# One bias group a step later, squares on ScalarE, and transposes of normalized rows moved beside the next tile's

## The chip, the core and the metric

The kernel runs on one core of a Trainium2 chip. The metric is the device time of one execution in microseconds (us). The kernel before takes 612.4 us, the median of three runs (612.08 to 612.52).

## The reference, cut to what matters

```python
scores = q @ k.T / sqrt(64)                       # (2, 8, 576, 576)
bias = relu(log1p(|i-j|) / log1p(max(i,1)) * w1 + b1) @ w2      # one per head
attn = softmax(scores + bias); x = attn @ v       # -> (1152, 512)
x = x / sqrt(mean(x*x, -1) + 1e-6) * rms_g
y = (silu(x @ w_gate) * (x @ w_val)) @ w_out      # weights in float64, cut to float32
out = (s * relu(y @ w_in)**2 + b) @ w_out2
```

## The kernel before

The instruction order of every engine is written by hand: each engine runs its own list in the order in which the Python code issues it, and waits only on semaphores. The attention stage is a loop over steps `s`. One step handles one unit, which is one pair of heads of one tile of 128 query rows; there are 9 tiles of 4 units (`r = s % 4`), so 36 units. The feed-forward layers come after it and take the larger part of the time.

In step `s` TensorE (PE) computes, in this order: the bias rows of one group of 16 query positions (`bias_mm`, line 188; a group is due some steps ahead of its use), the scores of unit `s+1` (line 243), three batches of transposes of the probabilities of unit `s` (`turn_mm`, called t0, t1 and t2 here, lines 271 and 273), the products of unit `s-1` with the values (line 300), and at certain `r` the transposes of a finished tile. VectorE (DVE) does the softmax sums (`soft`, line 255), the copy of t1 (line 279) and most hidden rows of the bias network (`hidden`, line 175). ScalarE (ACT) does the exponentials (line 262), the copies of t0 and t2 (line 279) and the bias rows (`br`, line 204), which travel through DRAM (`rows`) into the `bias` tile of a chunk of query positions.

A finished tile `p` passes these functions: `finish_a` copies the attention output out of PSUM (oT, line 306), `finish_t` transposes it on PE into a PSUM bank (line 313), `finish_b` scales it on VectorE by the softmax sums (ri, lines 319 and 320; x, line 322), `finish_s` sums its squares and takes the power -0.5 (lines 330 and 334), `finish_n` normalizes (line 339), and `finish_c` transposes the normalized rows on PE into a PSUM bank (line 345), from which ScalarE casts the high part `xs[0]` (line 348) and VectorE then subtracts to get the low part `xs[1]` (line 349). In the loop, `finish_a` and `finish_t` of tile `p` come at `r = 1`, `finish_b` and `finish_s` at `r = 2` of the next step, `finish_n` at `r = 3`, `finish_c` at `r = 0`.

All PSUM tiles named `b` come from one ring of three banks, in the order in which they are asked for; the bias rows of groups 8 and up, t0, t1, t2, and the two transposes of a finished tile share it. A fourth request takes the first one's bank again and has to wait until that one has been read:

```python
psB = ring(ctx, "psB", 3, space=PSUM)
```

Groups 32 to 35 have rows of over 512 columns and take two banks each; from step 25 on there are no bias groups any more.

Of the kernel before, what the change touches and what calls it, by code (L numbers as in the profile page):

```python
# [12 lines left out]
AF = mybir.ActivationFunctionType  # L13
ALU = mybir.AluOpType
# [9 lines left out]
NTT = 9  # L24
NT = B * S
DM = H * D
# [7 lines left out]
TILES = list(range(NTT))  # L34
POOL_QUAD = 3
ACT_QUAD = 2
ACT_EARLY = (0, 1, 2, 3, 4, 5, 6, 7, 10, 11)
SCALE = 8.0
AHD = 8
POOL_FROM = 12  # L40
# [10 lines left out]
def tile_kernel(ctx: ExitStack, tc: tile.TileContext, q, k, v, ltab, lg, cst, cst2, rms_g, wg, wv, wo, win, wo2, s_p, b_p, out):  # L51
    nc = tc.nc
# [70 lines left out]
    def load_q(p):  # L123
        if p < NTT:
            qt[p] = q_p.tile([P, NP, P], F32, name="q")
            nc.sync.dma_start(out=qt[p], in_=q[TILES[p]])

    def load_k(n):
        ks[n] = ac.tile([P, S], F32, name=f"ks{n}")
        nc.sync.dma_start(out=ks[n], in_=k[:, n])  # L130

    def load_v(n):
        t = ac.tile([P, 10, D], F32, name=f"vs{n}")
        nc.sync.dma_start(out=t, in_=v[:, n])
        vs[n] = t
# [10 lines left out]
    def keep_clock(n):  # L146
        warm = psB.tile([P, 512], F32, name="b")
        for _ in range(n):
            nc.tensor.matmul(warm[:, :P], ident, ident, start=True, stop=True)
# [13 lines left out]
    def hidden(g):  # L163
        hms[g] = []
        d = reach(g)
        for tq in range(4):
# [3 lines left out]
            hms[g].append(hq)  # L170
            if tq == ACT_QUAD and g in ACT_EARLY:
                nc.scalar.activation(hq, src, AF.Relu, bias=nthr[:, n:n + 1], scale=w1_sb)
# [19 lines left out]
    def bias_out(g, pb):  # L192
# [10 lines left out]
        for dst, src in parts:  # L203
            nc.scalar.activation(dst, src, AF.Identity, bias=cb[:, 1:2] if g in ACT_EARLY else cb[:, 0:1],  # L204
                                 scale=minv_sb[:, g:g + 1])
# [8 lines left out]
    def bias_in(g):  # L214
        qc, g16 = divmod(g, 8)
        if qc not in bias:
            bias[qc] = bias_p.tile([P, H, S], F32, name="bias")
        r = rows.pop(g)
        src = bass.AP(tensor=r.tensor, offset=r.offset + 15, ap=[[H * RW - 1, 16], [RW, H], [1, S]])
        for dst in ([0] if qc < 4 else [0, 64]):  # L220
            to = dst + (P if qc < 4 else D)
            nc.sync.dma_start(out=bias[qc][dst + g16:to:8 if qc < 4 else 4, :, :], in_=src)
# [11 lines left out]
    def scores_mm(u):  # L234
        hp = u % 4
        ps = [psA.tile([P, 2, 512], F32, name="a").rearrange("p f c -> p (f c)")[:, 512 - SPLIT:512 - SPLIT + S]
              for _ in range(2)]
        b = batches(u)
        for f in (slice(0, SPLIT), slice(SPLIT, S)):
            for e in range(2):  # L240
                for i in range(2):
                    ed, qc = slice(e * D, (e + 1) * D), slice(i * D, (i + 1) * D)
                    nc.tensor.matmul(ps[e][qc, f], qt[u // 4][ed, hp, qc], ks[b[i % len(b)] * NP + hp][ed, f],  # L243
                                     start=True, stop=True, tile_position=(e * D, i * D))
        return ps
# [58 lines left out]
    def finish_a(p):  # L304
        oT = xx_p.tile([P, DM], F32, name="oT")
        nc.scalar.copy(oT, pos.pop(p))
        fin[p] = oT

    def finish_t(p):
        oT = fin[p]  # L310
        px = psB.tile([P, 512], F32, name="b")
        for c in range(NKC):
            nc.tensor.transpose(px[:, c * P:(c + 1) * P], oT[:, c * P:(c + 1) * P], ident)
        fin[p] = oT, px

    def finish_b(p):
        oT, px = fin[p]
        ri = st_p.tile([P, H], F32, name="ri")
        nc.vector.tensor_scalar(ri, sums.pop(p), 1e-9, None, op0=ALU.add)
        nc.vector.reciprocal(ri, ri)  # L320
        x = xx_p.tile([P, DM], F32, name="x")
        nc.vector.tensor_tensor(out=x.rearrange("p (h d) -> p h d", h=H),
                                in0=px.rearrange("p (h d) -> p h d", h=H),
                                in1=ri.unsqueeze(2).to_broadcast([P, H, D]), op=ALU.mult)
        fin[p] = oT, x

    def finish_s(p):
        oT, x = fin[p]
        ss = st_p.tile([P, 1], F32, name="ss")
        nc.vector.tensor_tensor_reduce(out=oT, in0=x, in1=x, scale=1.0 / DM, scalar=1e-6,  # L330
                                       op0=ALU.mult, op1=ALU.add, accum_out=ss)

        rstd = st_p.tile([P, 1], F32, name="rstd")
        nc.gpsimd.tensor_tensor(out=rstd, in0=ss, in1=mh, op=ALU.pow)
        fin[p] = x, rstd
# [5 lines left out]
    def finish_c(p):  # L341
        x = fin.pop(p)[0]
        pxt = psB.tile([P, 512], F32, name="b")
        for c in range(NKC):
            nc.tensor.transpose(pxt[:, c * P:(c + 1) * P], x[:, c * P:(c + 1) * P], ident)
        src = pxt.rearrange("p (c t) -> p c t", c=NKC)
        cs = slice(p * P, (p + 1) * P)
        nc.scalar.copy(xs[0][:, :, cs], src)
        nc.vector.tensor_tensor(out=xs[1][:, :, cs], in0=src, in1=xs[0][:, :, cs].bitcast(F32), op=ALU.subtract)
# [28 lines left out]
    def bits_of(n):  # L378
        raw, a = wst[n]
        w = wst[n] = wpools["ab"].tile([P, 4 * P], I32, name="ww")  # L380
        yield nc.vector.tensor_scalar(a, a, 3, 0x3FFFFFF8, op0=ALU.logical_shift_left, op1=ALU.bitwise_and)  # L381
        yield nc.vector.scalar_tensor_tensor(out=w, in0=raw[:, :, 1], scalar=-0x40000000, in1=a,  # L382
                                             op0=ALU.bitwise_and, op1=ALU.bitwise_or)
        yield nc.vector.scalar_tensor_tensor(out=w, in0=raw[:, :, 0], scalar=29, in1=w,  # L384
                                             op0=ALU.logical_shift_right, op1=ALU.bitwise_or)
# [15 lines left out]
    NU = 4 * NTT  # L401
    NG = S // 16
    plan = {s: [] for s in range(-2, NU + 4)}
    plan[-2] = list(range(AHD))
    for g in range(AHD, NG):
        plan[g - 11 if g > 11 else -1].append(g)

    def hide(g):
        if g < NG:
            hidden(g)  # L410
# [12 lines left out]
    def groups(s):  # L423
        for g in plan[s]:
            pb = bias_mm(g)
            bias_out(g, pb)
            if s == -1 and g == AHD:
                hide(11)
            if s == -2:
                hide(g + LEAD)  # L430

    for s in range(-2, NU + 1):
        r = s % 4
        if s >= 5 and r == 1:
            finish_a(s // 4 - 1)
        if s >= 0 and r == 0:
            load_q(s // 4 + 1)
        if -1 <= s < 5:
            load_k(s + 3)
        if 0 <= s < 7:  # L440
            load_v(s + 1)
        landed = list(rows)[:2 if s > 3 else 1]
        if s != -1:
            groups(s)
        for g in landed:
            bias_in(g)
        if s >= 6 and r == 2:
            finish_b(s // 4 - 1)
        if s in BITS:
            part = bits_of(BITS[s])  # L450
        if 0 <= s + 1 < NU:
            ps = scores_mm(s + 1)
            if s == -1:
                groups(s)
                keep_clock(3)
            soft(s + 1, 0, ps[0])
        next(part, None)
        if 0 <= s < NU:
            turn_out(s, 0, turn_mm(s, 0))
        if 0 <= s + 1 < NU:  # L460
            expo(s + 1, 0)
            soft(s + 1, 1, ps[1])
        next(part, None)
        if 0 <= s < NU:
            for e in (1, 2):
                turn_out(s, e, turn_mm(s, e))
        if 0 <= s + 1 < NU:
            expo(s + 1, 1)
        next(part, None)
        if s >= 6 and r == 2:  # L470
            finish_s(s // 4 - 1)
        if s >= 7 and r == 3:
            finish_n(s // 4 - 1)
        if s >= -1:
            hide(s + 13)
        if s == 4:
            nc.sync.dma_start(out=s_sb, in_=s_p)
            nc.sync.dma_start(out=b_sb, in_=b_p)
        if 0 <= s - 1 < NU:
            values_mm(s - 1)  # L480
        if s >= 5 and r == 1:
            finish_t(s // 4 - 1)
        if s == 6:
            xs = [act_p.tile([P, NKC, NT], F32R, name=f"xs{i}", tag=f"x{i}") for i in range(2)]
        if s >= 8 and r == 0:
            finish_c(s // 4 - 2)
        if s == 26:
            gen.close()
            wpools["ab"] = ring(ctx, "wab", 2)
            wpools["sp"] = ring(ctx, "wsp", 4)  # L490
        for at, fn, n in TAIL:
            if at == s:
                fn(n)
        if s == 34:
            sco.close()
            psC = ring(ctx, "psC", 4, space=PSUM)
# [255 lines left out]
```

## Time and profile before

| what | value |
|---|---|
| median of three runs | 612.4 us (612.08 to 612.52) |
| profiled execution | 612.25 us, span of its instructions 610.5 us |
| granted TensorE clock | 1.00 of full speed |
| PE busy | 602.0 us (99% of the span) |
| VectorE, ScalarE, GpSimd busy | 407.8, 310.0, 191.2 us |
| start-up to the first t0 | 0 to 26.3 us |
| attention steps | 26.3 to about 180.4 us |
| feed-forward layers | 180.4 us to the end |

The span goes from the first to the last instruction; 1.75 us of the execution lie outside it. A busy PE says little by itself, since ends of matmuls are modelled; when each instruction starts says more. The idle time in square brackets in a timeline row is that of the engine just before the instruction, with what ended it.

### The profile page before, as it was taken

To read this page: it belongs to the slowest core of one execution; us is meant where nothing else is said; L and a number is where in the kernel's file an instruction comes from. 1 tells how busy PE (TensorE), PEld (TensorE's weight loads), DVE (VectorE), ACT (ScalarE), POOL (GpSimd) and SP (SyncE) were. 2 spreads that over 40 slices of the span, in tenths; PEclk is the share of its full clock that TensorE was granted. 3 is DMA by queue.
4 is the path that set the end of the run, shared out by engine and by line. 5 is a ranking of instruction groups with operands and counts; after the bars stand their busy time and mean duration, and the time that the engine had idled before them with its cause. 6 is when DMAs were issued, how large, how long until landed. Compare 5 with 4: busy or idle time off the path is not lost.

```text
span 610.5 us, 13370 instructions
## 1 busy us (share of the span) xinstructions
PE 602.0 (99%) x5430; PEld 540.2 (88%) x5430; DVE 407.8 (67%) x750; ACT 310.0 (51%) x646; POOL 191.2 (31%) x176
## 2 busy tenths in 40 slices
PE   8999999999999999999999999999999999999997
PEld 6466666667789999999999999999999999999997
DVE  7977999977878545654556355447887635788841
ACT  7887777777764443444434222335554335555210
POOL 0424235620113333234324223323224323332420
PEclk9999999999999999999999999999999999999999
DMA  7899545475112222132222222221223321122431
GB/s 216 245 306 250 162 139 153 143 210 146 37 39 104 71 103 69 70 104 96 77 70 83 91 104 77 96 68 71 69 70 105 117 91 68 71 70 70 143 100 53
DMA packets 25886, 67.54 MB, mean 111 GB/s; under 512 B 3136, under 2 KB 4704, under 8 KB 25824
## 3 DMA queue, kind: packets, MB, share of 16 engines
q1 hardware_dynamic: 25776, 66.66, 34.1%
q8 instruction: 43, 0.70, 0.5%
q14 instruction: 19, 0.16, 0.1%
q10 hardware_dynamic: 48, 0.02, 0.0%
HBM read 53.47 MB, written 10.83 MB: 105 GB/s over the span
## 4 chain that ended last, share of the span: by engine, by line
PE 76%; DVE 14%; ACT 5%; issue 3%; DMA 1%; POOL 1%; ACTq 0%; DVEq 0%; POOLq 0%
PE c L543 9%; PE c L544 9%; PE c L542 9%; PE b L544 7%; PE b L543 7%; PE b L542 7%; PE po L300 7%; PE a L243 6%; PE b L271 5%; DVE f L611 5%; DVE hv L607 4%; PE b L188 3%; ACT f L610 3%; PE po L543 2%; PE po L544 2%
## 5 line engine op out<-in xcount | busy, mean ns | idle before, releaser
L397 POOL TENSOR_TENSOR wlo<-ww,whi 128x512 fp32r<-128x512 f32 x68 | 95.7, 1408 | 102.9 <-ACT whi L396 102.9
L375 POOL TENSOR_SCALAR wa<-wa 128x512 f32<-128x512 f32 x68 | 44.0, 648 | 183.8 <-ACT wa L374 181.3
L381 DVE TENSOR_SCALAR wa<-wa 128x512 int32<-128x512 int32 x68 | 39.9, 587 | 42.7 <-POOL wa L375 42.7
L255 DVE CUSTOM_DVE_ANT_0 sn<-a,bias 128x576 f32<-128x576 f32 x72 | 51.8, 754 | 17.8 <-PE a L243 10.8
L374 ACT ACTIVATE wa<-wraw 128x512 f32<-128x512 f32 x68 | 45.3, 666 | 30.3 <-DMA wraw<-in_wo 27.3
L262 ACT ACTIVATE pr<-sn,nm 128x576 f32<-128x576 f32 x72 | 56.1, 780 | 3.4 <-DVE nm L255 3.4
L543 PE MATMUL c<-f,whi 128*128 128x384 f32 (+1 forms) x168 | 55.7, 332 | 0.0
L544 PE MATMUL c<-f,wlo 128*128 128x384 f32 (+1 forms) x168 | 55.7, 332 | 0.0
L542 PE MATMUL c<-f,whi 128*128 128x384 f32 (+1 forms) x168 | 55.7, 332 | 0.0
L175 POOL TENSOR_SCALAR hq<-tab,c_sb,thr 128x384 f32<-128x384 f32 (+17 forms) x24 | 45.2, 1892 | 30.1 <-PE b L188 30.1
L382 DVE SCALAR_TENSOR_TENSOR ww<-wraw,wa 128x512 int32<-128x512 int32 x68 | 51.7, 761 | 3.5 <-ACT f L653 0.4
L611 DVE SCALAR_TENSOR_TENSOR f<-hv,b_sb,f 128x384 fp32r<-128x384 f32 x48 | 39.3, 819 | 21.9 <-ACT f L610 21.9
L384 DVE SCALAR_TENSOR_TENSOR ww<-wraw,ww 128x512 int32<-128x512 int32 x68 | 52.2, 767 | 2.2
L610 ACT ACTIVATE f<-hv,b_sb 128x384 fp32r<-128x384 f32 x48 | 29.6, 617 | 45.1 <-DVE hv L607 45.0
L396 ACT CAST whi<-ww 128x512 fp32r<-128x512 f32 x68 | 41.7, 614 | 13.8 <-DVE ww L384 8.6
L543 PE MATMUL c<-xs,whi 128*128 128x384 f32 x144 | 48.2, 335 | 0.0
L542 PE MATMUL c<-xs,whi 128*128 128x384 f32 x144 | 48.2, 335 | 0.0
L544 PE MATMUL c<-xs,wlo 128*128 128x384 f32 x144 | 48.1, 334 | 0.0
L300 PE MATMUL po<-pt,vs 128*32 128x128 f32 (+1 forms) x1600 | 47.2, 264 | 0.1
L243 PE MATMUL a<-ks,q 64*64 64x352 f32 (+1 forms) x576 | 44.8, 416 | 0.5 <-ACT br L204 0.4
L544 PE MATMUL b<-f,wlo 128*128 128x384 f32 (+1 forms) x132 | 44.8, 339 | 0.5 <-POOL wlo L397 0.5
L543 PE MATMUL b<-f,whi 128*128 128x384 f32 (+1 forms) x132 | 44.6, 338 | 0.0
(122 smaller groups left out, 1478.2 us busy)
## 6 DMA issues: line engine op xcount, KB each, us to landing
wraw<-in_wo SPq DMA_DIRECT2D x28, 512.0 KB, 3.5
bias<-rows SPq DMA_DIRECT2D x32, 288.0 KB, 4.2
rows<-br SPq DMA_DIRECT2D x28, 295.5 KB, 3.0
wraw<-in_win SPq DMA_DIRECT2D x16, 512.0 KB, 3.5
wraw<-in_wg SPq DMA_DIRECT2D x12, 512.0 KB, 3.5
wraw<-in_wv SPq DMA_DIRECT2D x12, 512.0 KB, 3.5
vs<-in_v SPq DMA_DIRECT2D x8, 320.0 KB, 7.0
ks<-in_k SPq DMA_DIRECT2D x8, 288.0 KB, 6.3
```

The lines of the kernel that those rows point to most:

```text
L243: nc.tensor.matmul(ps[e][qc, f], qt[u // 4][ed, hp, qc], ks[b[i % len(b)] * NP + hp][ed, f], start=True, stop=True, tile_position=(e * D, ...
L255: nc.vector.tensor_tensor_reduce(out=sn, in0=ps, in1=bias[chunk(u)][:, h, :], scale=-1.0 / SCALE, scalar=3.0e38, op0=ALU.add, op1=ALU.min, ...
L262: nc.scalar.activation(prs[u][:, e * S:(e + 1) * S], sn, AF.Exp, bias=nm, scale=-1.0, accum_out=sums[u // 4][:, h:h + 1])
L300: nc.tensor.matmul(dst, w, a, start=c == 0, stop=c == NQC - 1, tile_position=(0, o))
L382: yield nc.vector.scalar_tensor_tensor(out=w, in0=raw[:, :, 1], scalar=-0x40000000, in1=a, op0=ALU.bitwise_and, op1=ALU.bitwise_or)
L384: yield nc.vector.scalar_tensor_tensor(out=w, in0=raw[:, :, 0], scalar=29, in1=w, op0=ALU.logical_shift_right, op1=ALU.bitwise_or)
L397: nc.gpsimd.tensor_tensor(out=lo, in0=w.bitcast(F32), in1=hi.bitcast(F32), op=ALU.subtract)
L542: nc.tensor.matmul(ps, hi[:, ws], ah, start=first, stop=False)
L543: nc.tensor.matmul(ps, hi[:, ws], al, start=False, stop=False)
L544: nc.tensor.matmul(ps, lo[:, ws], ah, start=False, stop=last)
L610: nc.scalar.activation(hh[:, cols(j)], g2, AF.Identity, bias=b_sb)
L611: nc.vector.scalar_tensor_tensor(out=hl[:, cols(j)], in0=g2, scalar=b_sb, in1=hh[:, cols(j)].bitcast(F32), op0=ALU.add, op1=ALU.subtract)
```

## The change

Three things change. Group 11 of the bias rows, the twelfth, is computed in step 0 and no longer in step -1, and its third quarter of hidden rows goes from ScalarE to VectorE. The sum of squares in `finish_s` is an activation of ScalarE with an accumulator, followed by a small GpSimd instruction that divides by 512 and adds 1e-6, where VectorE did all this in one instruction. And `finish_c` of tile `p` is called one step later: at `r = 1`, right behind `finish_t` of tile `p+1` (at steps 9, 13, 17, 21, 25, 29 and 33), with tile 7 staying at step 36 and tile 8 in the feed-forward part.

```diff
-ACT_EARLY = (0, 1, 2, 3, 4, 5, 6, 7, 10, 11)
+ACT_EARLY = (0, 1, 2, 3, 4, 5, 6, 7, 10)
...
     def finish_s(p):
         oT, x = fin[p]
         ss = st_p.tile([P, 1], F32, name="ss")
-        nc.vector.tensor_tensor_reduce(out=oT, in0=x, in1=x, scale=1.0 / DM, scalar=1e-6,
-                                       op0=ALU.mult, op1=ALU.add, accum_out=ss)
-
+        nc.scalar.activation(oT, x, AF.Square, accum_out=ss)
+        nc.gpsimd.tensor_scalar(ss, ss, 1.0 / DM, 1e-6, op0=ALU.mult, op1=ALU.add)
...
     for g in range(AHD, NG):
-        plan[g - 11 if g > 11 else -1].append(g)
+        plan[g - 11 if g > 10 else -1].append(g)
...
         if s >= 5 and r == 1:
             finish_t(s // 4 - 1)
+        if s >= 9 and r == 1:
+            finish_c(s // 4 - 2)
...
-        if s >= 8 and r == 0:
-            finish_c(s // 4 - 2)
+        if s == NU:
+            finish_c(NTT - 2)
```

The lists of the engines show how the order moves. In the changed file the lines from 334 to the main loop have a number lower by one, so line 345 is 344 and line 349 is 348.

TensorE, from the oT transposes of step 21 to the probabilities of step 22, before. The rows `b` of line 188 are the two banks of group 33 (512 and 32 columns):

```order
L313 MATMUL b<-ident,oT 128x128 [waits Activation_49]
L313 MATMUL b<-ident,oT 128x128 x3
L188 MATMUL b<-hq,c_sb 32x512 [waits DVE_49]
L188 MATMUL b<-hq,c_sb 32x512 x2
L188 MATMUL b<-hq,c_sb 32x512 [waits Pool_49]
L188 MATMUL b<-hq,c_sb 32x32 [waits Activation_49]
L188 MATMUL b<-hq,c_sb 32x32 x3
L243 MATMUL a<-ks_721,q 64x352 x4
L243 MATMUL a<-ks_721,q 64x224 x4
L271 MATMUL b<-ident,pr 128x128 [waits DVE_49]
```

And the same piece in the changed kernel:

```order
L313 MATMUL b<-ident,oT 128x128 [waits Activation_49]
L313 MATMUL b<-ident,oT 128x128 x3
L344 MATMUL b<-ident,x 128x128 [waits DVE_49]
L344 MATMUL b<-ident,x 128x128 x3
L188 MATMUL b<-hq,c_sb 32x512 [waits Activation_49]
L188 MATMUL b<-hq,c_sb 32x512 x2
L188 MATMUL b<-hq,c_sb 32x512 [waits Pool_49]
L188 MATMUL b<-hq,c_sb 32x32 [waits DVE_49,PE_49]
L188 MATMUL b<-hq,c_sb 32x32 x3
L243 MATMUL a<-ks_721,q 64x352 x4
L243 MATMUL a<-ks_721,q 64x224 x4
L271 MATMUL b<-ident,pr 128x128 [waits PE_49]
```

Four transposes stand in between, with a bank of their own, so every later request of the ring meets another predecessor: the second bank of the group (32 columns) takes the bank of the oT transposes, and waits for VectorE.

VectorE, from the hidden rows at the end of step 9 to the softmax of step 10, before:

```order
L175 TENSOR_SCALAR hq<-tab,c_sb,thr 128x368 x3
L319 TENSOR_SCALAR ri<-rs 128x8
L320 RECIPROCAL ri<-ri 128x8 [waits DVE_49]
L322 TENSOR_TENSOR x<-b,ri 128x512 [waits DVE_49,PE_49]
L255 ISA sn,nm<-a,bias 128x576 [waits PE_49,Activation_49]
```

And in the changed kernel:

```order
L175 TENSOR_SCALAR hq<-tab,c_sb,thr 128x368 x3
L348 TENSOR_TENSOR xs_981<-b,xs_980 128x4x128 [waits Activation_49]
L319 TENSOR_SCALAR ri<-rs 128x8
L320 RECIPROCAL ri<-ri 128x8 [waits DVE_49]
L322 TENSOR_TENSOR x<-b,ri 128x512 [waits DVE_49]
L255 ISA sn,nm<-a,bias 128x576 [waits PE_49]
```

The subtraction of the low part, which waits for ScalarE's cast, now stands ahead of the scaling that empties the bank of the oT transposes.

ScalarE, around the first exponentials (`pr`, of unit 0), before; `br` 128x400 and 128x191 are the two parts of group 11:

```order
L204 ACTIVATE br<-b,cb,c_sb 128x416 [waits DMAHW7_49,PE_49,Activation_49]
L204 ACTIVATE br<-b,cb,c_sb 128x175
L204 ACTIVATE br<-b,cb,c_sb 128x400 [waits DMAHW0_49,PE_49,Activation_49]
L204 ACTIVATE br<-b,cb,c_sb 128x191
L262 ACTIVATE pr,rs<-sn,nm 128x576 [waits DVE_49] x2
L279 COPY pt_451<-b 128x512 [waits PE_49]
```

And in the changed kernel:

```order
L204 ACTIVATE br<-b,cb,c_sb 128x416 [waits DMAHW7_49,PE_49,Activation_49]
L204 ACTIVATE br<-b,cb,c_sb 128x175
L262 ACTIVATE pr,rs<-sn,nm 128x576 [waits DVE_49] x2
L204 ACTIVATE br<-b,cb,c_sb 128x400 [waits DMAHW0_49,PE_49,Activation_49]
L204 ACTIVATE br<-b,cb,c_sb 128x191
L279 COPY pt_451<-b 128x512 [waits PE_49]
```

The two exponentials change places with the two parts of group 11; the first copy of a turn stays behind both.

## Rows read from the trace of the kernel before

**Rows 1.** Windows cut at oT transposes: busy PE, PEld, DVE, ACT, POOL; clock, DMA.

```profile
67.78:85.72 17.94, 17.94 (x304) 11.62 (x301) 16.25 (x40) 14.41 (x35) 7.92 (x5) 1.00 0.51 152
104.09:123.04 18.95, 18.88 (x312) 11.88 (x308) 17.86 (x40) 14.65 (x36) 10.04 (x5) 1.00 0.47 142
156.30:171.46 15.16, 15.16 (x312) 11.00 (x308) 12.53 (x30) 10.79 (x28) 1.84 (x2) 1.00 0.10 37
```

**Rows 2.** Timeline, turn after oT transposes at 67.78: start, length, engine, line, operands.

```profile
68.36 0.80 PE L188 MATMUL b<-hq,c_sb 128*32 128x352 f32 x8
69.09 1.20 PE L243 MATMUL a<-ks,q 64*64 64x352 f32 x16
70.22 1.09 PE L271 MATMUL b<-ident,pr 128*128 128x128 f32 x8
```

**Rows 3.** Timeline: the late bias of the third tile and what follows.

```profile
57.30 0.76 DVE L255 CUSTOM_DVE_ANT_0 sn<-a,bias 128x576 f32<-128x576 f32 x1 [2.33 <-DMA rows<-br]
62.41 0.66 PE L345 MATMUL b<-ident,x 128*128 128x128 f32 x4
63.58 0.77 PE L188 MATMUL b<-hq,c_sb 128*32 128x336 f32 x8 [0.52 <-DVE pt L279]
```

**Rows 4.** Timeline: a bank freed late at step 20.

```profile
119.96 0.67 DVE L349 TENSOR_TENSOR xs<-b,xs 128x512 fp32r<-128x512 f32 x1
120.68 1.09 PE L271 MATMUL b<-ident,pr 128*128 128x128 f32 x8
```

**Rows 5.** Timeline: evacuation of transposed normalized rows, a turn without bias rows.

```profile
137.08 0.66 PE L345 MATMUL b<-ident,x 128*128 128x128 f32 x4
137.77 0.59 ACT L348 CAST xs<-b 128x512 fp32r<-128x512 f32 x1
138.39 0.69 DVE L349 TENSOR_TENSOR xs<-b,xs 128x512 fp32r<-128x512 f32 x1 [1.42 <-ACT xs L348]
139.00 0.75 DVE L255 CUSTOM_DVE_ANT_0 sn<-a,bias 128x576 f32<-128x576 f32 x1
```

**Rows 6.** Timeline, turn after oT transposes at 123.04 (two-bank bias group).

```profile
123.63 1.13 PE L188 MATMUL b<-hq,c_sb 128*32 128x512 f32 x16
124.06 0.17 DVE L319 TENSOR_SCALAR ri<-rs 128x8 f32<-128x8 f32 x1
124.56 0.69 DVE L322 TENSOR_TENSOR x<-b,ri 128x512 f32<-128x512 f32 x1
```

**Rows 7.** Timeline: score matmuls after the oT transposes of 85.72 and 104.09.

```profile
87.14 1.20 PE L243 MATMUL a<-ks,q 64*64 64x352 f32 x16
105.62 1.20 PE L243 MATMUL a<-ks,q 64*64 64x352 f32 x16
```

**Rows 8.** Timeline: VectorE's copy beside the oT transposes of 171.46.

```profile
171.57 0.68 DVE L279 COPY pt<-b 128x512 f32<-128x512 f32 x1
```

**Rows 9.** Timeline: squares, power and normalization of one tile.

```profile
108.93 0.68 DVE L330 CUSTOM_DVE_ANT_0 oT<-x 128x512 f32<-128x512 f32 x1
109.70 0.87 POOL L334 TENSOR_TENSOR rstd<-ss,mh 128x1 f32<-128x1 f32 x1 [9.36 <-DVE ss L330]
113.25 0.91 DVE L339 SCALAR_TENSOR_TENSOR x<-x,rstd,g_bc 128x512 f32<-128x512 f32 x1
```

**Rows 10.** Timeline: ScalarE and VectorE around the first softmax.

```profile
22.46 3.04 ACT L204 ACTIVATE br<-b,cb,c_sb 128x432 f32<-128x432 f32 x6
23.07 0.76 DVE L255 CUSTOM_DVE_ANT_0 sn<-a,bias 128x576 f32<-128x576 f32 x1 [1.04 <-DMA ks<-in_k]
25.35 0.81 ACT L262 ACTIVATE pr<-sn,nm 128x576 f32<-128x576 f32 x1
26.99 0.59 ACT L279 COPY pt<-b 128x512 f32<-128x512 f32 x1
```

**Rows 11.** Windows of two microseconds early on; columns as in rows 1.

```profile
24.00:26.00 2.00, 1.75 (x21) 1.13 (x19) 2.00 (x5) 2.00 (x5) 2.00 (x2) 1.00 0.70 267
28.00:30.00 2.00, 2.00 (x27) 0.85 (x20) 1.94 (x5) 2.00 (x7) 1.18 (x1) 1.00 1.01 310
```
## What I expected, before the run

> **What bounds the kernel now.** I read the windows first, cut where PE starts the oT transposes of a finished tile. From 67.78 to 85.72 us PE is busy for 17.94 of 17.94 us, and so again from 156.30 to 171.46; in the window from 104.09 it lacks 0.07 us, which is the one visible wait of that stretch [rows 1]. The granted clock is 1.00 throughout. VectorE is close behind (17.86 of 18.95 us), ScalarE has 3.5 us to spare in the first window. Since a busy PE can hide waits, I then read the timeline of PE in single steps: from one instruction group to the next the starts are the same in every turn, as 0.58 us for four transposes (67.78 to 68.36), 0.73 for a bias group, 1.13 for the scores [rows 2]. So in the attention steps PE sets the time, and what PE waits there is added to the end, unless it makes good a wait that is there already. Two such waits exist. The first follows the softmax of the third tile, which starts 2.33 us after VectorE came free, at 57.30, because its bias has not landed [rows 3]; the second is a bank that VectorE frees late at step 20 [rows 4].
>
> **The moved transposes: the new wait.** The amount of work on PE stays the same; 0.58 us of transposes leave step `r = 0` and appear at `r = 1`. What changes is who empties which bank. Call T the start of the oT transposes. PE now issues the oT transposes (T to T+0.58), the transposes of the normalized rows (to T+1.16), the bias group, the scores, t0. The list of VectorE has the subtraction into `xs[1]` ahead of `finish_b`, and the bank of the oT transposes comes free only with `finish_b`. From the start of the transposes of normalized rows to ScalarE's cast it is 0.69 us, from the cast to the subtraction 0.62, from there to VectorE's next instruction 0.61 [rows 5]; from `ri` to `x` 0.50, and `x` takes 0.69 [rows 6], after which I allow 0.05 for the signal, as from 120.63 to 120.68 [rows 4]. So the bank is free at T + 0.58 + 0.69 + 0.62 + 0.61 + 0.50 + 0.69 + 0.05 = T+3.74. Before, `finish_b` began as soon as VectorE had done its hidden rows, at T+1.02 in the turn of 123.04 [rows 6].
>
> When does PE want that bank? The ring has three, and the two transposes stand directly behind each other, so the bank goes to the second request after them.
> - Steps 9, 13, 17: the first is the next bias group, the second t0. Before, t0 began at 70.22, T+2.44 [rows 2]; with 0.58 more that is T+3.02, a wait of 0.72. In the next two turns the scores begin at 87.14 and 105.62, T+1.42 and T+1.53 [rows 7]; with 1.13 and 0.58 added t0 comes at T+3.13 and T+3.24: waits of 0.61 and 0.50.
> - Step 21: group 33 takes two banks, so its second bank is the one that waits. All 16 matmuls take 1.13 us [rows 6]; by columns (512 of 544) the first bank takes 1.06, so PE arrives at T+2.22 and waits 1.52. Bounds: 1.45 (if the first bank took all) and 2.58.
> - Steps 25, 29, 33: no bias group stands between, so t1 gets the bank. t0 comes at T+3.02 less the 0.73 of the bias group, T+2.29, t1 half of the 1.09 of t0 and t1 later [rows 2], at T+2.83: waits of 0.91. At step 33 the second transposes also need the bank of t1, which VectorE leaves at 172.25, T+0.79 instead of T+0.58 [rows 8]; that moves the whole chain by 0.21, so 1.12.
>
> Sum: 0.72 + 0.61 + 0.50 + 1.52 + 0.91 + 0.91 + 1.12 = 6.29 us. Each is lost whole, since PE has no idle time after it in which to make it good. Behind the waiting instruction stand the rest of the step's transposes, the values and the next scores; VectorE and ScalarE wait for those and gain air.
>
> **What the move gives back.** At step 8 PE is through with the values at 62.41, runs the transposes, and then the bias group waits for VectorE's copy until 63.58 [rows 3]. Without the transposes there that group takes the bank of t0, emptied earlier, and begins at 62.41: 63.58 - 62.41 - 0.58 = 0.59 us won. At step 20 the wait of t0 for the subtraction (120.63) goes [rows 4]; PE lacks 0.07 us in that window [rows 1], and I take 0.1.
>
> **The squares on ScalarE.** VectorE is rid of 0.68 us per tile [rows 9]. ScalarE gets an activation: the exponential of 576 columns takes 0.81 [rows 10], by columns 0.72 for 512, and about 0.2 for reading the accumulator, so 0.9. It delays the bias rows and copies of step `r = 3`; with 3.5 us to spare per tile [rows 1] I cost it at nothing. If that cover is gone, each tile loses up to about 0.45: the spare time is 3.5 us over four steps, 0.9 a step, and I suppose that half of it lies where the delay falls. GpSimd's added instruction on 128x1 has no row; I put it between nothing and the power's own 0.87. In the turn shown the power begins at 109.70 and the normalization at 113.25 [rows 9]: 0.9 later for ScalarE and 0.9 more for the added instruction, it would end at 112.4, so hidden either way.
>
> **Group 11 a step later.** ScalarE wrote three bias groups in 3.04 us ahead of the first exponential at 25.35 [rows 10]. With the third behind the exponentials, they start about 1.0 earlier, but the first copy of t0 still stands behind all of this; it came at 26.99. VectorE's softmax of the first half was done at about 23.8, so ScalarE's queue alone held the exponentials; I take 0.5 us as the gain (bounds 0 and 1.0). VectorE's added quarter of hidden rows falls into the 1.04 us that it idles before that softmax [rows 10]. SyncE's loads of step 0 no longer stand behind the store of group 11, which had to wait for ScalarE's rows until 25.50; the transfers were at 0.70 of their engines then, and at 1.01 shortly after [rows 11]: pulled ahead by some 1 us, they relieve the saturated stretch that makes the softmax at 57.30 late. If the late bias lands no earlier, PE's 0.5 is lost again there, so 0; if it lands early enough, 0.5 and most of the 0.9 us that PE waits for it, 1.4. I take the middle, 0.7.
>
> **Sum.** 6.29 - 0.59 - 0.1 - 0.7 = +4.9 us. Against the profiled execution of 612.25, which is 0.15 under the median of 612.4, that gives 617.2 us.
>
> **A rule against this.** Rows 3 show a group of matmuls that stands for 0.52 us because the third bank is not empty. The Trainium skill (Perfetto Trace Analysis, section Matmuls) says that independent matmul groups should rotate through different PSUM banks, so that emptying one overlaps the next group's matmuls; the two transposes do lie in different banks, and by that rule alone the moved work would be hidden. The first rival below is that case.
>
> **The rivals.**
> - Faster: the two banks are emptied beside the bias group and the scores. It decides if `finish_b` is through by about T+2.8 in place of T+3.74, so that the waits sum to under 1.4 us; then only the gains remain, 612.25 - 1.4 = 610.8, or 610.1 if the late bias gains fully. For it speaks that nothing waits there now. Against it: cast, subtraction and scaling are one chain of three engines' work, each with a row. 5 in 100.
> - No change: gains at their upper end and waits half hidden, for instance if t0's wait shortens because VectorE scales before the cast is through. The listed order excludes that. 4 in 100.
> - Slower by less: the chain is as said, but the wait at step 21 is small and the front gains 1.4; +3, 615.3. 13 in 100.
> - Slower by more: ScalarE, now with 0.9 us more per tile and the cast ahead of the bias rows, makes t2 wait for the bank of the bias group, 0.45 at each of seven tiles: 4.9 + 3.1, 620.3. For it: the delay falls in one step of four; against: with 14.41 + 0.9 it has 15.3 us of work in 17.94 [rows 1]. 13 in 100.
> - The forecast: 65 in 100.
>
> **How the numbers follow.** A measurement here tells a change of about 0.2% (1.2 us) from none. Slower by more than that: 65 + 13 + 13 = 91 in 100; the same 4; faster 5. The range takes in the smaller and larger slow cases: 614.8 to 620.3.
>
> **What would show it.** PE's first t0 after the moved transposes (at steps 25 and on, t1) waits for VectorE's `x` of line 322, with about 0.5 to 0.7 us, at step 21 the second bank of the bias group with 1.5, and seven such waits in all; the chain of work that ended last passes through ScalarE's cast, the subtraction and `finish_b` there. The wait at 63.58 is gone. The softmax of the third tile begins up to 1.4 us earlier. I am wrong if PE runs through at these places, or if the cast begins earlier than 0.69 behind the transposes.

## The result, and the profile after

The changed kernel takes 617.32 us (median of 4 runs, 615.54 to 618.05) against 612.24 before (611.62 to 612.52): a ratio of 1.0074, with a 95% interval of 1.0054 to 1.0093, so it is slower by 5.1 us. I had 617.2. Its profiled execution took 616.75 us, with a span of 614.6, so 4.1 us of span have to be found.

The waits of TensorE in the changed kernel; columns: engine, line waited for, us in total, times, the longest:

```profile
PE b L271 <- ACT pt L279: 2.4, 3, 0.8
PE b L271 <- DVE x L322: 1.7, 3, 0.7
PE b L188 <- DVE x L322: 1.5, 1, 1.5
...
PE b L344 <- DVE x L338: 0.3, 1, 0.3
...
PE b L344 <- DVE pt L279: 0.2, 1, 0.2
```

Seven waits of 5.6 us in total stand in the first three lines; the kernel before has none of these. That they fall where the forecast put them is read from the timeline. The wait for `x` of line 338 was not forecast: at step 36 the transposes of tile 7 wait 0.27 us for its normalization. e7 below has this wait too, e1, e3 and e4 have not; its cause is open. The turn that answers to [rows 2], from the oT transposes at 65.68 (T) on:

```profile
65.68 0.65 PE L313 MATMUL b<-ident,oT 128*128 128x128 f32 x4
...
66.17 0.60 PE L344 MATMUL b<-ident,x 128*128 128x128 f32 x4
66.70 0.80 PE L188 MATMUL b<-hq,c_sb 128*32 128x352 f32 x8
66.81 0.59 ACT L347 CAST xs<-b 128x512 fp32r<-128x512 f32 x1 [0.51 <-PE b L344]
67.43 0.69 DVE L348 TENSOR_TENSOR xs<-b,xs 128x512 fp32r<-128x512 f32 x1 [1.03 <-ACT xs L347]
67.43 1.20 PE L243 MATMUL a<-ks,q 64*64 64x352 f32 x16
68.03 0.16 DVE L319 TENSOR_SCALAR ri<-rs 128x8 f32<-128x8 f32 x1
...
68.47 0.69 DVE L322 TENSOR_TENSOR x<-b,ri 128x512 f32<-128x512 f32 x1
...
69.31 0.96 PE L271 MATMUL b<-ident,pr 128*128 128x128 f32 x7 [0.68 <-DVE x L322]
```

Read it downwards: the second transposes end, ScalarE casts, VectorE subtracts, then it begins `ri` and `x` for the other bank, and only when `x` ends at 69.16 does t0 start. VectorE stood idle for 1.03 us ahead of the subtraction, with the oT transposes long done: the wait is one of order, not of work. The bank came free at T+3.48 (forecast T+3.69, before the signal), and t0 started 0.15 us later, where 0.05 had been allowed for the signal.

At step 21, which answers to [rows 6], the bias group is torn in two, and its second bank waits:

```profile
122.91 1.07 PE L188 MATMUL b<-hq,c_sb 128*32 128x512 f32 x8
125.51 0.27 PE L188 MATMUL b<-hq,c_sb 128*32 128x32 f32 x8 [1.54 <-DVE x L322]
```

In a turn without bias rows it is t1 that waits:

```profile
143.95 0.66 PE L271 MATMUL b<-ident,pr 128*128 128x128 f32 x4
...
144.59 0.69 DVE L322 TENSOR_TENSOR x<-b,ri 128x512 f32<-128x512 f32 x1
144.70 0.59 ACT L279 COPY pt<-b 128x512 f32<-128x512 f32 x1 [1.19 <-PE b L271]
...
145.42 0.63 PE L271 MATMUL b<-ident,pr 128*128 128x128 f32 x4 [0.81 <-ACT pt L279]
```

Here the profile names ScalarE's copy as the releaser, and the name is a coincidence: that copy ends at 145.29 and `x` at 145.28. The copy is t0's, and t1 does not take its bank; e4 below shows that the wait goes with the order of the banks.

Third, the front, that is the steps up to about the second tile's oT transposes. The softmax of the third tile, at 57.30 in [rows 3], begins at 56.20, and the bias group of step 9 at 61.19 where it stood at 63.58:

```profile
56.20 0.76 DVE L255 CUSTOM_DVE_ANT_0 sn<-a,bias 128x576 f32<-128x576 f32 x1 [3.04 <-DMA rows<-br]
```

```profile
61.19 0.75 PE L188 MATMUL b<-hq,c_sb 128*32 128x336 f32 x8
```

Where the 4.1 us of span come from is read from the starts of the oT transposes, turn by turn; a turn is the stretch from one tile's oT transposes to the next tile's:

| from the start of the oT transposes | before | after | difference |
|---|---|---|---|
| start of the first | 48.66 | 47.46 | -1.20 |
| first to second | 19.12 | 18.22 | -0.90 |
| second to fifth (three waits) | 55.26 | 56.20 | +0.94 |
| fifth to sixth (step 21) | 18.11 | 19.92 | +1.81 |
| sixth to eighth (two waits) | 30.31 | 32.02 | +1.71 |
| eighth to the feed-forward start | 8.91 | 10.30 | +1.39 |
| feed-forward part | 430.13 | 430.48 | +0.35 |

Two rows have to be read with the moved transposes in mind. The stretch from the first start to the second loses a group of 0.58 us altogether, since the group now stands behind the second start; it comes back in the stretch from the eighth start on, which holds two such groups where it held one. So the front is 1.20 and 0.32 us shorter, not 1.20 and 0.90.

### The profile page after: what moved, and what is told of

It reads as the page before. It is cut to its first block, busy times and chain, and to the rows that moved or that the text cites. A ratio compares the mean times of both kernels' runs of the same rounds, so it can differ in the third digit from the quotient of the medians.

```text
span 614.6 us, 13385 instructions
## 1 busy us (share of the span) xinstructions
PE 602.3 (98%) x5430; PEld 540.4 (88%) x5430; DVE 402.8 (66%) x733; ACT 314.4 (51%) x663; POOL 192.5 (31%) x185
## 4 chain that ended last, share of the span: by engine, by line
PE 72%; DVE 15%; ACT 8%; issue 3%; POOL 1%; DMA 1%; ACTq 0%; POOLq 0%; DVEq 0%
PE c L544 8%; PE c L545 8%; PE c L543 8%; PE b L545 6%; PE b L544 6%; PE b L543 6%; PE po L300 6%; PE a L243 6%; PE b L271 5%; DVE f L612 5%; DVE hv L608 4%; ACT f L611 3%; PE b L188 3%; DVE ww L381 2%; PE po L544 2%
## 5 line engine op out<-in xcount | busy, mean ns | idle before, releaser
L271 PEld LDWEIGHTS b<-ident,pr 128*128 128x128 f32 x288 | 30.7, 140 | 16.7 <-issue 7.3
```

What stands on the lines that cost most here:

```text
L271: nc.tensor.transpose(pT[:, c * P:(c + 1) * P], pr[:, o:o + P], ident)
```

## The experiments

The theory: the moved transposes take the next bank of a ring of three, VectorE empties the second of the two banks first, and PE waits for the first. Rivals: the squares slow ScalarE; or the work added at `r = 1` is the cost, whatever the order. In the edits `...` stands for unchanged lines. Each kernel was timed beside the kernel before.

| run | edit | us (runs) | ratio to before (95% interval) |
|---|---|---|---|
| e1 | before, only `finish_c` moved | 617.56 (4) | 1.0082 (1.0060 to 1.0104) |
| e2 | before, only group 11 later | 610.81 (10) | 0.9988 (0.9969 to 1.0008) |
| e3 | before, only the squares moved | 613.44 (10) | 1.0021 (1.0011 to 1.0030) |
| e4 | changed, the two transposes swapped | 611.44 (10) | 0.9981 (0.9971 to 0.9991) |
| e5 | e4 with the squares on VectorE | 610.32 (12) | 0.9963 (0.9950 to 0.9975) |
| e6 | e4 with the last tile's squares on VectorE | 610.81 (12) | 0.9977 (0.9964 to 0.9989) |
| e7 | changed, the subtraction behind `finish_b` | 611.14 (12) | 0.9979 (0.9965 to 0.9992) |
| e8 | e2 with the loads of step 0 behind the store | 613.86 (12) | 1.0020 (1.0004 to 1.0035) |
| e9 | e5 with those loads in step -1 | 609.74 (8) | 0.9961 (0.9946 to 0.9975) |

### One part at a time (e1, e2, e3)

Each takes one hunk of the change and leaves the others out.

```diff
+        if s >= 9 and r == 1:
+            finish_c(s // 4 - 2)
...
-        if s >= 8 and r == 0:
-            finish_c(s // 4 - 2)
+        if s == NU:
+            finish_c(NTT - 2)
```

e1: 

> The kernel before with nothing changed but the place of finish_c (group 11 and the squares stay as they were). If the bank of the oT transposes is the cause, all seven waits are here: +6.3 us of waits, -0.7 for the wait that goes at step 8 and the one at step 20, so 612.2 + 5.6 = about 617.8 us, with PE waiting for line 322's x at steps 10, 14, 18, 22, 26, 30, 34. If instead ScalarE's squares slow the step, this kernel stands at 611.5 us.

Measured 617.56 us: the whole loss is in the move. PE's waits are the same seven, with 2.4, 1.7 and 1.5 us.

```diff
-ACT_EARLY = (0, 1, 2, 3, 4, 5, 6, 7, 10, 11)
+ACT_EARLY = (0, 1, 2, 3, 4, 5, 6, 7, 10)
...
-        plan[g - 11 if g > 11 else -1].append(g)
+        plan[g - 11 if g > 10 else -1].append(g)
```

e2: 

> The kernel before with group 11 a step later and nothing else. My theory: the front gain comes from here, PE's first oT transposes begin about 1.2 us earlier (as in the changed kernel: 47.46 against 48.66) and the third tile's softmax about 1.1 us earlier, so 612.2 - 1.1 = 611.1 us. The rival (the front gain comes from VectorE being rid of the squares at step 6) gives 612.2 us here.

Measured 610.81 us, but the interval of the ratio takes in 1. The traces say more about the first start. The first oT transposes begin at 47.77 here, with the squares still on VectorE, and between 47.46 and 48.15 in the changed kernel, e4 to e7 and e9, which all have the group a step later; without that change they begin at 48.66 (before), 48.97 (e1) and 48.71 (e3, the squares alone). So the earlier first start is the group's. How much of it lasts is not shown: the third tile's softmax begins at 56.78 and the second oT transposes at 67.07 (67.78 before), but single executions scatter here by about as much. The kernel before and e1 issue the same work up to that softmax and begin it at 57.30 and 58.72.

```diff
-        nc.vector.tensor_tensor_reduce(out=oT, in0=x, in1=x, scale=1.0 / DM, scalar=1e-6,
-                                       op0=ALU.mult, op1=ALU.add, accum_out=ss)
+        nc.scalar.activation(oT, x, AF.Square, accum_out=ss)
+        nc.gpsimd.tensor_scalar(ss, ss, 1.0 / DM, 1e-6, op0=ALU.mult, op1=ALU.add)
```

e3: 

> The kernel before with the squares on ScalarE and GpSimd and nothing else. My theory: hidden, 612.2 us within 0.3, PE's waits as before. The rival (ScalarE's 0.9 us per tile delays bias rows and copies): up to 0.45 at seven tiles, 615.3 us. If the squares help VectorE where it is nearly full, 611.8 us.

Measured 613.44 us: a miss. The squares are not hidden; they cost some 1.2 us (0.7 to 1.8 by the interval). Part of the place is in the trace of e3, at the last tile, which is finished in the feed-forward part:

```profile
185.27 0.63 ACT L330 ACTIVATE oT<-x 128x512 f32<-128x512 f32 x1 [1.44 <-DVE x L322]
185.81 0.19 ACT L330 ACTIVATION_READ_ACCUMULATOR oT<-x 128x1 f32 x1
186.09 0.19 POOL L331 TENSOR_SCALAR ss<-ss 128x1 f32<-128x1 f32 x1 [6.56 <-ACT oT L330]
186.36 0.56 POOL L333 TENSOR_TENSOR rstd<-ss,mh 128x1 f32<-128x1 f32 x1
186.95 0.75 DVE L338 SCALAR_TENSOR_TENSOR x<-x,rstd,g_bc 128x512 f32<-128x512 f32 x1 [1.79 <-ACT sg L564]
...
192.03 0.68 DVE L348 TENSOR_TENSOR xs<-b,xs 128x512 fp32r<-128x512 f32 x1
...
192.76 0.44 PE L542 MATMUL c<-xs,whi 128*128 128x384 f32 x1 [0.36 <-DVE xs L348]
```

The normalization of the last tile waits for ScalarE's square and two GpSimd instructions, the low part is done at 192.71, and the matmul that reads it had waited for 0.36 us. The kernel before has no such wait, and its feed-forward part takes 430.13 us against 430.43 in e3.

### The order of the two banks (e4, e7)

```diff
+        if s >= 9 and r == 1:
+            finish_c(s // 4 - 2)
         if s >= 5 and r == 1:
             finish_t(s // 4 - 1)
-        if s >= 9 and r == 1:
-            finish_c(s // 4 - 2)
```

e4: 

> The changed kernel with one edit: at r = 1 the transposes of the normalized rows are issued ahead of the oT transposes, so that the two take each other's bank, in the order in which VectorE empties them. If the order of emptying is the cause, the first bank is free at about T+2.0 and the second at about T+3.2, before PE wants either (T+3.0 and T+3.5 with a bias group, T+2.8 and T+3.3 without one): six or seven of the waits vanish, 617.3 - 6.0 = about 611.2 us. If the cause is the added work at r = 1 on VectorE and ScalarE, whatever the bank, it stays at 617 us.

Measured 611.44 us: four lines in another order take back 5.9 us. PE has no wait for line 322 any more; 0.2 us ahead of the second transposes at step 33 stay. The same turn in e4:

```profile
66.08 0.66 PE L344 MATMUL b<-ident,x 128*128 128x128 f32 x4
66.57 0.60 PE L313 MATMUL b<-ident,oT 128*128 128x128 f32 x4
66.77 0.59 ACT L347 CAST xs<-b 128x512 fp32r<-128x512 f32 x1
67.10 0.80 PE L188 MATMUL b<-hq,c_sb 128*32 128x352 f32 x8
67.39 0.69 DVE L348 TENSOR_TENSOR xs<-b,xs 128x512 fp32r<-128x512 f32 x1 [0.58 <-ACT xs L347]
67.83 1.20 PE L243 MATMUL a<-ks,q 64*64 64x352 f32 x16
...
68.51 0.69 DVE L322 TENSOR_TENSOR x<-b,ri 128x512 f32<-128x512 f32 x1
68.96 1.09 PE L271 MATMUL b<-ident,pr 128*128 128x128 f32 x8
```

VectorE does the same instructions in the same order as in the changed kernel. But t0 starts without a wait, at 68.96, while `x` still runs to 69.20: t0 has the bank that the subtraction left at 68.08, and `x` is done when t1 wants the other. The rival that the added work itself is the cost falls.

e7 keeps PE's order and changes VectorE's instead:

```diff
+        low[p] = src, cs
...
+    def finish_d(p):
+        src, cs = low.pop(p)
         nc.vector.tensor_tensor(out=xs[1][:, :, cs], in0=src, in1=xs[0][:, :, cs].bitcast(F32), op=ALU.subtract)
...
             finish_b(s // 4 - 1)
+        if s >= 10 and r == 2:
+            finish_d(s // 4 - 2)
```

e7: 

> The changed kernel, its order on PE untouched (oT transposes first), but VectorE's subtraction of the low part is issued behind the scaling of finish_b in the next step. If VectorE's order holds the bank, the bank of the oT transposes is free at about T+2.3 and the other at T+3.0, and all seven waits go but a rest at step 21 (under 0.2): about 611.4 us, as with the swapped transposes. If PE's order of the transposes is what counts, it stays at 617 us.

Measured 611.14 us. In its trace `x` precedes the subtraction, and t0 starts on time:

```profile
66.23 0.80 PE L188 MATMUL b<-hq,c_sb 128*32 128x352 f32 x8
...
66.78 0.69 DVE L322 TENSOR_TENSOR x<-b,ri 128x512 f32<-128x512 f32 x1 [0.47 <-DVE ri L320]
66.96 1.20 PE L243 MATMUL a<-ks,q 64*64 64x352 f32 x16
...
67.39 0.68 DVE L354 TENSOR_TENSOR xs<-b,xs 128x512 fp32r<-128x512 f32 x1
68.09 1.09 PE L271 MATMUL b<-ident,pr 128*128 128x128 f32 x8
```

A wait of 0.4 us stays for the second bank at step 21 (under 0.2 expected). So it is neither engine's order alone: the order in which VectorE empties the two banks has to be that in which PE fills them.

### The squares (e5, e6)

e5 has in `finish_s` the lines of before; e6 takes them for the last tile alone:

```diff
+        if p == NTT - 1:
+            nc.vector.tensor_tensor_reduce(out=oT, in0=x, in1=x, scale=1.0 / DM, scalar=1e-6,
+                                           op0=ALU.mult, op1=ALU.add, accum_out=ss)
+        else:
...
```

e5: 

> Group 11 a step later and the moved transposes with the swapped order of the run before, but the squares stay on VectorE in one instruction. My theory: the squares on ScalarE cost about 0.35 us in the feed-forward part (the last tile's low part comes later) and up to 0.3 in the attention steps, so 611.4 - 0.6 = about 610.8 us, and PE's wait for the low part (0.4 us) is gone. If the squares pay on VectorE's full steps, this is slower than the swapped kernel: over 611.8 us.

e6: 

> The swapped kernel with the squares of the last tile alone back on VectorE. If the chain of the last tile (ScalarE, two GpSimd instructions, then the normalization, cast and low part) is the price of the squares, PE's wait of 0.4 us for the low part goes and the time falls by 0.35 to about 611.1 us. If the price lies in the attention steps it stays at 611.4.

Measured 610.32 and 610.81 us, beside 611.44 for e4. In both PE's wait of 0.4 us for the low part is gone. The order e4, e6, e5 is the expected one, but the intervals of e4 and e6 overlap almost wholly, and the feed-forward part takes 430.56 us in e4, 430.41 in e6 and 430.00 in e5. So the wait at the last tile is shown, and what it is worth is not. The intervals of e4 and e5 (0.9971 to 0.9991, 0.9950 to 0.9975) share only their ends; with e3 that says that the squares belong on VectorE here. Another part of their price is in the turn from the fifth to the sixth tile, which takes 18.32, 18.35 and 18.34 us in e3, e4 and e6, with these squares on ScalarE, and 18.11 and 18.14 in the kernel before and e5, with them on VectorE: 0.2 us. In e3 it is at the last bias group, which takes 1.29 us to the start of the scores (132.59 to 133.88) against 1.08 before (132.50 to 133.58). What the rest of their price is stays open.

### The front (e8, e9)

```diff
         landed = list(rows)[:2 if s > 3 else 1]
+        if s == 0:
+            groups(s)
         if s >= 0 and r == 0:
             load_q(s // 4 + 1)
...
-        if s != -1:
+        if s > 0 or s == -2:
             groups(s)
```

e8: 

> Group 11 a step later, nothing else, and SyncE's loads of step 0 are issued behind the store of group 11 as in the kernel before. If the loads that go ahead are what lets the third tile's bias land earlier, that softmax is back at about 57.3 us (56.8 with the loads ahead) and the time at 611.6 us; if only ScalarE's queue counts, the softmax stays at 56.8 and the time at 610.8 us.

Measured 613.86 us, far beyond 611.6. The loads matter more than I had thought: the keys themselves come too late, three times, and the third tile's softmax moves to 59.45:

```profile
41.57 1.20 PE L243 MATMUL a<-ks,q 64*64 64x352 f32 x16 [1.20 <-DMA ks<-in_k]
46.39 1.20 PE L243 MATMUL a<-ks,q 64*64 64x352 f32 x16 [0.72 <-DMA ks<-in_k]
51.51 0.82 PE L243 MATMUL a<-ks,q 64*64 64x352 f32 x8 [0.33 <-DMA ks<-in_k]
```

The first of the loads of step 0, as SyncE issues them in the kernel before, in e2 and in e8:

```profile
25.89 0.45 SPq L126 DMA_DIRECT2D q<-in_q  x1
24.30 0.42 SPq L126 DMA_DIRECT2D q<-in_q  x1
27.11 0.42 SPq L126 DMA_DIRECT2D q<-in_q  x1
```

The first oT transposes follow in the same order, at 48.66, 47.77 and 49.88. So the front gain needs the loads ahead of the store of group 11: with the same computing order and the store ahead, moving the group was a loss. But e8 issues the loads later than even the kernel before, since that store now waits for rows that are computed later. It shows that the loads matter, and does not measure their share of the gain.

```diff
-        if s >= 0 and r == 0:
+        if s > 0 and r == 0:
             load_q(s // 4 + 1)
...
+        if s == -1:
+            load_q(1)
+            load_k(3)
+            load_v(1)
```

e9: 

> The fastest kernel so far (group 11 later, swapped transposes, squares on VectorE) with SyncE's three loads of step 0 issued in step -1, ahead of the stores of the bias groups 8 to 10. If early free transfer time is what the third tile's bias needs, its softmax begins at about 55.8 us (56.55 without this) and the time falls by up to 0.7 to 609.6 us. The rival: the loads then compete with the first bias stores, the first softmax (23.07 us) and first t0 (25.6 us) come later by up to 1 us, and the time is 610.3 us or more.

Measured 609.74 us. The third tile's softmax comes at 55.42 (56.55 in e5), but the first one at 23.50 (23.02 in e5), and the first t0 at 26.11 (25.64 in e5). That looks like both theories at once, but e7, whose loads are not early, has 55.75 and 23.47, so neither shift is clear of the scatter. The first oT transposes come no earlier (48.15), and the ratio 0.9961 cannot be told from e5's 0.9963. By their medians e5 and e9 are the fastest kernels here, 0.37% and 0.39% under before.

## Why the prediction was right

**The new wait.** Right in place, mechanism and number: seven waits, for `x` of line 322, at t0 three times, at the second bank of the group once, at t1 three times. Forecast 0.72, 0.61, 0.50, 1.52, 0.91, 0.91, 1.12; the profile shows 0.68, 0.57, 0.46, 1.54, 0.81, 0.82 and 0.82, the last with another 0.21 ahead of the second transposes. The sum is 5.9 us against 6.29. These figures count from the modelled end of the group before. From start to start, as the forecast counted, and against the same two starts where nothing waits, the seven cost 0.75, 0.64, 0.53, 1.74, 1.00, 1.00 and 1.00, and the second transposes of step 33 another 0.37: 7.0 us, so the term was somewhat too small. e1 shows that they come from the move alone, e4 and e7 that the order of emptying is their cause.

**"The amount of work on PE stays the same."** That was wrong by a small amount, and in the kernel's favour. Three of the turns with a wait (second to fifth start) grew by 0.94 us, although 1.92 of waits, from start to start, lie in them. Most of the rest is in the hardware section below; 0.1 is the wait at step 20 that went, as forecast.

**What the move gives back.** The wait at 63.58 went as forecast: from the values to the bias group it is 1.12 us (60.07 to 61.19) in place of 2.41 (61.17 to 63.58), that is 0.58 for the moved transposes, the forecast 0.59, and 0.12 which the hardware section explains. The first start came 1.20 us earlier, where 0.7 was taken within bounds of 0 and 1.4; to the second start 0.32 more are left beside the forecast 0.59, since t2 of step 9 comes 0.27 late (64.19). Both together, 1.5 against 1.3, differ by less than single executions scatter, so the traces do not show that the front was mis-sized. What the loads add to a better place in ScalarE's queue is not measured apart; e2 and e8 show that they matter. And the two waits that I named were not all: the kernel before has two more of t0 and t1 for an exponential, of 0.55 us at 26.30 and 0.27 at 176.52, and neither is left in the changed kernel.

**The squares at nothing.** This term failed. e3 measures +1.2 us. Its trace has a wait of 0.36 us in the feed-forward part, at the last tile, where no attention step covers the longer chain, and 0.2 us at the last bias group in the loop, which the 3.5 us of spare time per tile did not cover. I had looked only at the tiles in the loop, and there only at an average. GpSimd's added instruction took 0.19 us. This cost and the larger waits did not spoil the sum because other misses ran the other way, above all PE's work, which became cheaper by about 0.26 us at each of four tiles. So the mechanism, the sign and the seven waits were foreseen, and that 617.2 came within 0.2 of 617.32 is partly luck.

**The rivals.** The faster one falls with the result and with e1. Two transposes in different banks still left 0.46 to 1.54 us of wait, and e4 and e7 show the overlap once the banks are emptied in the order in which they are filled. The Trainium skill (Perfetto Trace Analysis, section Matmuls) says that groups should rotate through different banks so that emptying one overlaps the next group's matmuls; this case agrees only under that condition of order. The slower one, ScalarE delaying t2 at seven tiles, does not show. Apart from the waits of t1, t2 comes more than 0.1 us late once in the changed kernel, by the 0.27 at step 9. In e5, with the squares on VectorE, the same t2 comes 0.56 late, so the squares are not its cause.

## What to carry to other kernels

With a small ring of buffers, count who gets the freed buffer, and in which order its readers release: two producers that stand next to each other need readers in the same order. When a group of work is moved to another step, follow its stores in the DMA queue too: which transfers stand ahead of them and which behind can decide whether the move gains or loses. And a chain that is covered in a loop has to be looked at once more at the last iteration, where the cover is gone.

## What the hardware showed beyond that

Transposes that follow transposes are cheaper than those between other matmuls. In [rows 2] four take 0.58 us, and the values ahead of transposes take 1.23 us to the next start against 1.11 ahead of a bias group, as two places in the trace of before show:

```profile
71.36 1.30 PE L300 MATMUL po<-pt,vs 128*32 128x128 f32 x40
72.47 0.80 PE L188 MATMUL b<-hq,c_sb 128*32 128x368 f32 x8
...
79.60 1.30 PE L300 MATMUL po<-pt,vs 128*32 128x128 f32 x40
80.83 0.66 PE L345 MATMUL b<-ident,x 128*128 128x128 f32 x4
```

In e5, where nothing waits in this turn, two groups stand together:

```profile
66.41 0.65 PE L345 MATMUL b<-ident,x 128*128 128x128 f32 x4
66.90 0.60 PE L313 MATMUL b<-ident,oT 128*128 128x128 f32 x4
67.43 0.80 PE L188 MATMUL b<-hq,c_sb 128*32 128x352 f32 x8
```

Together they take 1.02 us where two single groups took 1.16. With the 0.12 of the values that makes 0.26 us per tile, and the turn from the second oT transposes to the third indeed takes 17.66 us in e5 (66.90 to 84.56) against 17.94 in [rows 1]. This holds for the tiles whose turns have bias groups. Later the scores follow the values, which take 1.23 us to the next start there too (144.00 to 145.23 before), so only the 0.14 of the pair is left: the turn from the sixth tile to the seventh takes 15.00 us in e7 (138.38 to 153.38) against 15.15 before (141.15 to 156.30). In e5 it takes 15.14, for there t2 comes about 0.1 late and the gain is gone.
